# A fixed list of tasks in the place of a planner: block-sparse attention and a gated feed-forward on one core

## The chip, the cores and the metric

The kernel runs on one core of a Trainium2 chip. The core has five engines that work side by side, each through its own instructions in order: TensorE (PE, matrix products, with its weight loads shown as PEld), VectorE (DVE), ScalarE (ACT), GpSimd (POOL) and SyncE (SP, which here issues most of the DMAs). They meet only through semaphores. The metric is the device time of the program in microseconds: the median of 3 runs is 301.85 us (301.69 to 302.9).

## The reference

The input is `q`, `k`, `v` of 4 batches, 8 heads, 768 positions and 64 dimensions, in float32. The positions are cut into 24 blocks of 32. A block of queries sees its own block and the two neighbours, the first and the last block, and three sampled blocks; the first and last block of queries see all.

```python
scores = scale * np.matmul(q, k.transpose(0, 1, 3, 2))
mask = np.abs(blk_i - blk_j) <= window
mask = mask | (blk_i == 0) | (blk_j == 0) | (blk_i == n_blocks - 1) | (blk_j == n_blocks - 1)
for qb in range(n_blocks):
    for kb in sampled_blocks[qb]:
        mask[qb * block:(qb + 1) * block, kb * block:(kb + 1) * block] = True
scores = np.where(mask, scores, -1000000000.0)
attn = np.exp(scores - np.max(scores, axis=-1, keepdims=True))
attn = attn / (np.sum(attn, axis=-1, keepdims=True) + 1e-09)
x = np.matmul(attn, v)          # then (3072 tokens) x (512)
h = x @ w_in                    # 512 -> 2048
g = h * (1.0 / (1.0 + np.exp(-beta * h)))
out = (g @ w_out).astype(np.float32)
```

## The kernel before

The work is cut into tasks: one function each that issues a few instructions on one engine. A task is known by a name, and the numbers behind the name say which piece it is.

**Attention.** The 22 middle blocks of a batch are taken two at a time: 11 pairs a batch, 44 pairs in all, numbered 0 to 43 (`n`). A pair goes through these tasks:

- `kg`, `kn` gather the keys that the pair sees into the tile `KG` (POOL; `kn` on POOL or DVE). `KG` has 3 buffers.
- `vv`, `vg` gather its values into `VG` with DMAs that SP issues; `pick` and `pickv` do it for the sampled blocks of pairs 0 to 3 with PE, because the values are not yet in DRAM.
- `sc` computes mask and scores on PE (`emit_sm` L849, `emit_ss` L862: small products that use quarters of the array, "32-column tiles"). It takes two of the eight PSUM banks.
- `mx` (DVE, L884) takes the maxima, `ex` (ACT, L892) the exponentials and their sums, one task for each of two heads' halves.
- `hl` or `rc` (DVE) invert the sums. From pair 11 on `nrm` (POOL, L915) multiplies the exponentials by them; pairs 0 to 10 put the factor in later (`rs`, L953, L986).
- `tp` transposes on PE (L929), `ptv` copies the result out of PSUM. From pair 31 on one DMA on SP, `tpd` (L933), does both.
- `av` multiplies by the values (L953 and L971 up to pair 15, L963 from pair 16), and `xv` writes the result into `xT`, the feed-forward's input.

The first and last blocks of a batch go through `gs`, `gm`, `ge`, `gr`, `gn`, `gt`, `gptv`, `gav`, `gx` in the same way (L1026 to L1097). Before a batch's pairs, `ldV`, `ldK`, `ldQ` load its data in halves, `cast` turns batch 0's into float16, `trK`, `trQ` (L632) transpose keys and queries with 12 products of 64 columns for two heads, and `evK`, `evQ` copy them out of PSUM.

**Feed-forward.** The tokens are taken in eight groups (`G`) of 256, 256, 256, 512, 512, 512, 512 and 256. `h` (L1155) makes one of 16 slices of the hidden layer for a group, `tanh` (ACT, L1161) and `stt` (DVE, L1166) the gate, `y` (L1182) a quarter of the second product for 128 tokens, `oe` (ACT) copies the result out, `od` writes it to DRAM. The weights come in by POOL's DMAs `win` and `wout`. The gate's results `g` have two buffers; the second one, `g1`, is also lent to the values of pairs 4 to 7.

**The order.** `Plan.run` (L65) is a planner: it follows the dependencies with a duration for each task, and whenever an engine is free it takes the ready task of the lowest rank (its priority and a tuned correction, `OFFSET`). It also chooses the engine of a task that may run on two, and the PSUM bank of a task that opens one. The instructions are then written in the planned order, each engine's in that order. What the planner got wrong shows as an engine that waits: an engine never passes its next instruction by. When PE goes from products that use the whole array to products that use parts of it, or back, it first empties the array; the planner knows this as `CHANGE`.

The names that the change touches: `QV` (L260: what the load of the queries waits for), `TWO` (L268: from which pair on two pairs' scores are one task), `emit_tr` (L628), the casts (L538), `w_in`'s loads (L557), `emit_kg` (L703), the place of `g` (L1146), and the last eviction (L1200 to L1207).

## Time and profile before

| | |
|---|---|
| median of 3 runs | 301.85 us (301.69 to 302.9) |
| the profiled execution: its time, and its span | 302.9 us, 302.9 us |
| busy: PE, DVE, ACT, POOL | 279.5, 237.5, 218.6, 170.0 us |
| instructions: PE products, DVE, ACT, POOL | 4109, 556, 641, 513 |
| moved by DMA | 47.55 MB, of which 11.27 MB by POOL's queue |

The profiled execution is the slowest of the three runs. PE's busy time is modelled: products run into one another, so a slice in which PE is "full" need not be one in which the products follow each other as fast as they can. How fast they can is seen from the start of one to the start of the next. The same holds in small for the other engines: an instruction's last tenth of a microsecond lies under the next one's start.

### The profile page before, as it was taken

The page shows a single profiled execution, that of the slowest core. Times are in us where ns is not written, and L with a number is a line of the kernel's source. Part 1 is how long each engine was busy: PE and PEld are TensorE (multiplying, and loading weights), DVE is VectorE, ACT ScalarE, POOL GpSimd, SP SyncE. Part 2 cuts the span into 40 slices and gives each one's busy share as a digit, 9 for nine tenths or more (in the row PEclk, how much of TensorE's full clock was granted, in tenths as well). Part 3 has the DMA queues.
Part 4 walks back from the last instruction along what each step waited for, and adds up shares of the span by engine and source line. Part 5 has one row for each costly group of instructions (what it writes and reads, how often), then busy time and mean ns, then how long its engine had stood idle before and what let it go on. Part 6 is the DMA issues. An engine that isn't in the chain of part 4 may idle for free.

```text
span 302.9 us, 11451 instructions
## 1 busy us (share of the span) xinstructions
PE 279.5 (92%) x4109; PEld 173.8 (57%) x4109; DVE 237.5 (78%) x556; ACT 218.6 (72%) x641; POOL 170.0 (56%) x513
## 2 busy tenths in 40 slices
PE   2599879999998799999999999999999999999993
PEld 1465668758846576665556555545554544555671
DVE  5848987999899998999999739999888834762150
ACT  3357657888789598799889749896787768763360
POOL 5057995034579957899777538677976654000000
PEclk9999957999999999999999999999999999999999
DMA  7999999979978852299933643248465446541102
GB/s 248 365 294 171 205 232 231 228 142 265 213 126 167 181 192 72 84 173 162 237 99 106 202 154 106 67 110 167 120 158 119 126 106 181 137 121 53 53 36 69
DMA packets 57170, 47.55 MB, mean 157 GB/s; under 512 B 19733, under 2 KB 53142, under 8 KB 57114
## 3 DMA queue, kind: packets, MB, share of 16 engines
q1 hardware_dynamic: 44736, 35.48, 41.3%
q0 software_dynamic: 12320, 11.27, 24.7%
q8 instruction: 32, 0.52, 0.7%
q14 instruction: 24, 0.20, 0.2%
q10 hardware_dynamic: 58, 0.07, 0.1%
HBM read 45.23 MB, written 9.44 MB: 180 GB/s over the span
## 4 chain that ended last, share of the span: by engine, by line
PE 49%; DVE 23%; issue 7%; ACT 6%; POOL 6%; DMA 5%; POOLq 2%; SPq 0%; DVEq 0%; ACTq 0%
PE bank L1155 17%; PE bank L1182 14%; DVE ST L884 5%; PE bank L825 4%; DVE g L1166 4%; PE bank L929 3%; POOL KG L710 3%; DMA g<-in_k_dram 3%; DVE SG L1040 3%; POOL PP L915 2%; PE bank L963 2%; PE bank L971 2%; ACT PP L892 2%; PE bank L632 2%; ACT t L1161 2%
## 5 line engine op out<-in xcount | busy, mean ns | idle before, releaser
L1155 PE MATMUL bank<-xT,w_in_sb 128*128 128x256 f16 (+1 forms) x512 | 93.8, 330 | 1.5 <-DVE g L1166 1.5
L892 ACT ACTIVATE PP<-bank,ST 128x256 f16<-128x256 f32 x176 | 81.9, 482 | 15.1 <-DVE ST L884 10.1
L1182 PE MATMUL bank<-w_out_sb,g 128*128 128x512 f16 x384 | 92.0, 379 | 0.0
L1161 ACT ACTIVATE t<-bank,beta_sb 128x512 f16<-128x512 f32 (+1 forms) x128 | 71.0, 595 | 15.7 <-PE bank L1155 10.4
L915 POOL TENSOR_SCALAR PP<-PP,ST 128x256 f16<-128x256 f16 x132 | 63.4, 499 | 30.8 <-DVE ST L909 29.2
L1166 DVE SCALAR_TENSOR_TENSOR g<-t,bank 128x512 f16<-128x512 f16 (+1 forms) x128 | 67.0, 547 | 16.3 <-ACT t L1161 15.8
L1155 PEld LDWEIGHTS <-w_in_sb 128*128 128x128 f16 x512 | 54.4, 115 | 28.1 <-issue 4.1
L710 POOL COPY KG<-KT 128x64 f32 x264 | 52.4, 249 | 25.6 <-PE bank L862 10.5
L884 DVE TENSOR_REDUCE ST<-bank 128x2 f32<-128x512 f32 x88 | 57.6, 680 | 4.2 <-PE bank L862 3.8
L1182 PEld LDWEIGHTS <-g 128*128 128x128 f16 x384 | 35.0, 98 | 37.4 <-issue 3.5
L892 ACT ACTIVATION_READ_ACCUMULATOR PP<-bank,ST 128x1 f32 x176 | 37.4, 212 | 0.0
L1061 POOL TENSOR_SCALAR PG<-PG,SG 128x768 f16<-128x768 f16 x13 | 13.1, 1010 | 24.4 <-ACT PG L1049 15.2
L334 ACT ACTIVATE osb<-bank 128x512 f32<-128x512 f32 (+1 forms) x24 | 14.2, 590 | 16.1 <-PE bank L1182 16.0
L330 DVE COPY PT<-bank 128x1024 f16<-128x1024 f16 x30 | 20.4, 683 | 3.8 <-PE bank L929 3.6
L330 DVE CAST xT<-bank 64x256 f16<-64x256 f32 (+1 forms) x35 | 14.6, 418 | 9.9 <-PE bank L963 6.8
L929 PE MATMUL bank<-identity,PP 128*128 128x128 f16 x248 | 20.4, 225 | 1.2 <-ACT KT L328 0.6
L963 PEld LDWEIGHTS <-VG 128*128 128x128 f16 x448 | 16.1, 98 | 9.2 <-issue 4.3
L1049 ACT ACTIVATE PG<-bank,SG 128x384 f16<-128x384 f32 x32 | 18.3, 589 | 4.2 <-DVE SG L1042 3.6
L929 PEld LDWEIGHTS <-PP 128*128 128x128 f16 x248 | 16.2, 101 | 6.0 <-issue 1.1
L963 PE MATMUL bank<-PT,VG 128*128 128x64 f16 x448 | 17.5, 193 | 2.2 <-DMA PT<-PP 1.5
L330 POOL COPY KG<-KT 128x384 f32<-128x384 f32 (+3 forms) x43 | 16.6, 411 | 1.3 <-PE bank L862 1.3
L328 ACT CAST xT<-bank 64x256 f16<-64x256 f32 (+1 forms) x30 | 11.3, 375 | 8.2 <-PE bank L1089 3.9
(119 smaller groups left out, 317.9 us busy)
## 6 DMA issues: line engine op xcount, KB each, us to landing
VG<-VT SPq DMA_DIRECT2D x220, 32.0 KB, 2.6
VG<-VT SPq DMA_DIRECT2D x32, 192.0 KB, 2.7
out_dram<-osb SPq DMA_DIRECT2D x20, 256.0 KB, 2.1
RV<-in_v_dram POOLq DMA_DIRECT2D x6, 384.0 KB, 6.6
RK<-in_k_dram POOLq DMA_DIRECT2D x6, 384.0 KB, 6.2
VT<-Vn SPq DMA_DIRECT2D x3, 768.0 KB, 3.4
RQ<-in_q_dram POOLq DMA_DIRECT2D x6, 384.0 KB, 6.3
w_in_sb<-in_moe_w_in_dram POOLq DMA_DIRECT2D x8, 256.0 KB, 8.8
```

The costliest lines, as they stand in the source:

```text
L330: (nc.vector if eng == "DVE" else nc.gpsimd).tensor_copy(out=out, in_=in_)
L710: nc.gpsimd.tensor_copy(out=kg32[:, g, :, (SR + r) * W:(SR + r + 1) * W], in_=kt32[:, :, bass.ds(vals[3 * g + r], W)])
L884: mx[n, u] = add(f"mx{n}.{u}", "DVE", 0.6, lambda n=n, u=u, sb_=sb_: nc.vector.tensor_reduce(out=sb_[:, 0, 2 * u:2 * u + 2], in_=bank(("S" ...
L892: nc.scalar.activation(out=pb[:, u, g, :], in_=bank(("S", n, u))[:, g * 256:(g + 1) * 256], func=AF.Exp, bias=sb_[:, 0, 2 * u + g:2 * u + ...
L915: (nc.vector if eng == "DVE" else nc.gpsimd).tensor_scalar(out=pb[:, u, g, :], in0=pb[:, u, g, :], scalar1=sb_[:, 2, 2 * u + g:2 * u + g + ...
L929: nc.tensor.transpose(out=o[:, s * P:(s + 1) * P], in_=pb[:, u, g, c * P:(c + 1) * P], identity=identity)
L963: nc.tensor.matmul(o[:, (g * NHP + hp) * 2 * BLK:(g * NHP + hp + 1) * 2 * BLK], lhsT=vgb[:, g, c, hp * P:(hp + 1) * P], rhs=pt[:, g, c, :, ...
L1049: nc.scalar.activation(out=pg[:, :].rearrange("x (j p) -> x j p", j=J)[:, :, hf * hw_:(hf + 1) * hw_], in_=bank(("GS", m, hf))[:, 0:S // 2 ...
L1155: nc.tensor.matmul(o[:, 0:TW], lhsT=w_in_v[:, c, f // 4, f % 4, :], rhs=xT[:, c, c0:c0 + TW], start=(c == 0), stop=(c == NHP - 1))
L1161: lambda G=G, f=f, TW=TW, tt=tt: nc.scalar.activation(out=tt[:, 0:TW], in_=bank(("H", G, f))[:, 0:TW], func=AF.Tanh, bias=0.0, scale=beta_ ...
L1166: lambda G=G, f=f, TW=TW, tt=tt, gg=gg: nc.vector.scalar_tensor_tensor(out=gg[:, f, 0:TW], in0=tt[:, 0:TW], scalar=1.0, in1=bank(("H", G, ...
L1182: nc.tensor.matmul(o[:, :], lhsT=gg[:, f, s * P:(s + 1) * P], rhs=w_out_sb[:, f, :], start=(f == 0), stop=(f == N_FFC - 1))
```

## The change

The planner is gone. In its place stands a list, `ORDER`, of 1,727 words: all tasks in the order of writing, with the engine behind the name where a task may run on two (`:A` ACT, `:D` DVE, `:G` POOL) and the PSUM banks where it opens some (`:02`). `Plan.run` only reads the list. Durations that the planner used were also edited in many tasks; they have no effect on the program any more, and those lines are left out below.

With the list come these edits:

- Six `fill` tasks: products of zeros in float32 on PE, with no reader (6, 1, 4, 1, 1 and 2 products, each 128 rows by 256 columns), into a bank that is free at that point.
- Batch 0's casts write two heads side by side, so that its `trK`, `trQ` are 6 products of 128 columns that use the whole array. A cast may run on ACT: 3 of the 8 do.
- `QV`: the load of the queries no longer depends on the first copies of the values. In the list its second half, `ldQ0.1`, stands behind `vtab0.1` and `vtab0.0` on SP.
- `TWO` goes from 33 to 11: from pair 11 on, two neighbouring pairs of a batch have their masks and scores as one task (15 such tasks in the place of 5), which takes four banks at once.
- The register loads of the first four `kg` are tasks of their own, ahead (`kl0` to `kl3`).
- `win`: eight loads of one of the four row groups by half of the columns, in the place of two row groups by a quarter. `h` waits for the four of its half.
- `g` of group 1 lies beside that of group 0 in the first buffer, group 2's in the second. `VG`'s two halves of a pair lie apart.
- A list of row numbers that nothing read (8 POOL, 4 PE and 1 DVE instructions) is gone.
- The last eviction is one instruction on ACT; it was split between ACT and DVE.
- Other engines by the list: `ptv` 21 on DVE and 10 on ACT (before 30 and 1), `nrm` 27 on POOL and 6 on DVE (33 and 0), `xv` without the first eleven pairs 23 on DVE and 38 on ACT (35 and 26), `evK` 1 on DVE and 15 on ACT (4 and 12), `vres` 6 on DVE and 3 on POOL (9 and 0), `kn` 13 on DVE and 31 on POOL (17 and 27).

```diff
+ORDER = """
+sbl iota ldV0.1 ident ldK0.1 ldV0.0 id32 ldK0.0 ldQ0.0 idx kl0 mask.0 kl2 warm mask.1 selc srow kl3 fill6:1 selb0:0
+mask.2 castK0.3:A selb1:1 kl1 table vperm0.1 maskb:2 trK0.3:3 castK0.2:D vtab0.1 selw0 vperm0.0 fill1:5 trK0.2:4 selw1
+evK0.2:A maskc vtab0.0 sel16.4 sel16.3 ldQ0.1 castK0.0:A sel16.2 castK0.1:D fill4:5 trK0.0:4 sel16.1 trK0.1:2 sel16.5
...
+evQ0.1:A kn2:D vg2.2 kg0 evQ0.0:A vg0.2 kn1:D pick1.0:3 vg2.1 vg0.0 castQ0.3:A castQ0.2:D kg2 vg0.1 trQ0.2:2 beta
+trQ0.3:0 evQ0.2:D pick0.0:5 evQ0.3:A pickv1.0:D touch2 wout3.1 pickv0.1:D sc0:02 touch1 pickv0.0:A win1.0 sc1:36 mx0.0
...
+ex5.0 kg7 gm0 sc6:43 pickv2.0:A ge1 av2:0 hl4 win0.3 mx6.1 ge0 tp3:1 kn9:G rs2:D ldV1.0 xv1.0 ex6.1 sc7:26 gr0 vv8
+mx6.0 tp4:5 gn0:G ptv3:A gr1 kn10:G vg5.5 mx7.0 gt0:3 ex6.0 vg7.2 ldK1.1 mx7.1 vg5.3 xv2.0 gn1:G ex7.0 vg8.5 hl6
+fill2:7 gs2:1740 vg6.1 kn8:G gptv0 ptv4:A vg5.4 tp5:2 kg8 gm2 vg7.3 av3:3 ex7.1 vg5.2 vg5.1 av4:5 hl5 ge2 vg6.0 gm3
+win1.3 gt1:6 vg6.6 kg9 vg9.2 rs3:A trK1.1:1 gr2 rs4:A vg6.4 trQ1.0:7 xv3.0 ge3 xv4.0 tp6:3 gptv1 ldQ1.1 h0.1:5
...
+mx20.1 av18:1 vg20.5 tp19:5 vg19.6 mx21.1 tanh2.6 h2.11:4 vg19.3 tanh2.4 stt2.6 y1.0.1 kg24 vg22.3 ex21.1 ptv19:D
...
+y7.1.3 oe7.1 od7.1ACT od7.1SP
+"""
...
     def run(self):
...
+        by = {t.name: t for t in self.tasks}
+        full = dict(A="ACT", D="DVE", P="PE", G="POOL", S="SP")
         order = []
...
+        for word in ORDER.split():
+            name, _, place = word.partition(":")
+            if name.startswith("fill"):
+                k, i = int(name[4:]), int(place)
+                order.append(Task("fill", "PE", 0.43 * k, lambda k=k, i=i: self.fill(k, i)))
...
+            t = by[name]
+            t.eng = full[place[0]] if place and place[0] in full else next(iter(t.on))
...
-    QV = (0, 2)
+    QV = (0, 0)
...
-    TWO, TWOP = 33, 1
+    TWO, TWOP = 11, 1
...
+    def emit_fill(k, i):
+        for _ in range(k):
+            nc.tensor.matmul(banks[i][:, 0:256], lhsT=heat, rhs=heat[:, :].rearrange(
+                "x (a m) -> x a m", a=1).to_broadcast([P, 2, P]), start=True, stop=True, skip_group_check=True)
...
+                    if b == 0:
+                        for j in range(J):
+                            nc.tensor.transpose(out=o[:, j * P:(j + 1) * P],
+                                                in_=mixed(s16)[:, j, hp * P:(hp + 1) * P], identity=identity)
+                        return
...
-        gi = (G + (sizes[0] < 8)) % NG if G or sizes[0] >= 8 else 0
-        gc = TW if G == 1 and sizes[0] < 8 else 0
+        gi, gc = ((0, 0), (0, 256), (1, 0), (0, 0), (1, 0), (0, 0), (1, 0), (0, 0))[G]
...
-                te.emit, te.on = lambda ob=ob, G=G, s=s: scale_on(
-                    "ACT", ob[:, 0:256], bank(("Y", G, s))[:, 0:256], 0.5), {"ACT": 0.35}
-                tf = add(f"of{G}.{s}", "DVE", 0.35, lambda ob=ob, G=G, s=s: scale_on(
-                    "DVE", ob[:, 256:512], bank(("Y", G, s))[:, 256:512], 0.5), deps=list(te.deps), prio=te.prio,
-                    closes=(("Y", G, s),))
```

More of the change, by code (lines that the diff above doesn't have):

```diff
@@ L2 @@
-import heapq
 from contextlib import ExitStack
@@ L65, in run @@
     def run(self):
-        tasks = self.tasks
-        attention_left = sum(1 for t in tasks if t.opens and not t.moe)
-        succ = {}
-        need = {}
-        for t in tasks:
-            need[t] = len(t.deps)
-            for d in t.deps:
-                succ.setdefault(d, []).append(t)
-        readers = {}
-        for t in tasks:
-            for b in t.closes:
-                readers[b] = readers.get(b, 0) + 1
-        ready_at = {t: 0.0 for t in tasks}
-        engines = sorted({e for t in tasks for e in t.on})
@@ L80, in run @@
-        free = {e: 0.0 for e in engines}
-        waiting = {e: [] for e in engines}
-        ring_at = hw_at = 1.0
-        lanes = [0.0] * 8
-        issued = 0
-        tiling = 0
-        off = {t: t.prio + self.OFFSET.get(t.name, self.OFFSET.get(t.name.split(".")[0], self.OFFSET.get(t.kind, 0.0)))
-               for t in tasks}
-        def rank(t, e):
-            young = now - ready_at[t] < self.YOUNG[e] - 1e-9
-            return off[t] + (self.KEEP if e == "PE" and t.tiling != tiling else 0.0) + (self.YIELD if young else 0.0)
@@ L214, in run @@
+        assert sum(t.name != "fill" for t in order) == len(self.tasks) and all(b in self.bank for t in order for b in t.opens)
         return order
@@ L553 @@
     THR = 4.5
-    for fq in range(4):
-        fs = slice(fq * FQ * P, (fq + 1) * FQ * P)
-        for c in range(0, 4, 2):
-            t_win.append(add(f"win{fq}.{c // 2}", "POOL", 0.6, lambda c=c, fs=fs: nc.gpsimd.dma_start(
-                out=w_in_sb[:, c:c + 2, fs], in_=w_in_r[:, c:c + 2, fs]),
-                deps=[touch[fq // 2]], prio=-50 + 0.2 * fq + 0.05 * c, dma=1.3, bulk=THR))
+    for f in range(2):
+        fs = slice(f * D_FF // 2, (f + 1) * D_FF // 2)
+        for c in range(NHP):
+            t_win.append(add(f"win{f}.{c}", "POOL", 0.6, lambda c=c, fs=fs: nc.gpsimd.dma_start(
+                out=w_in_sb[:, c, fs], in_=w_in_r[:, c, fs]),
+                deps=[touch[f]], prio=-50 + 0.4 * f + 0.05 * c, dma=1.5, bulk=THR))
     for c in range(4):
@@ L840, in emit_vres @@
                 copy_on(eng, o, i.to_broadcast([BLK, 2, 2, D_MODEL]))
-            vres = add(f"vres{n}", {"POOL": 2.1, "DVE": 0.62}, None, emit_vres,
+            vres = add(f"vres{n}", {"POOL": 2.1, "DVE": 0.72}, None, emit_vres,
                        deps=vg[n - p] + ([av[vlast(n)]] if vlast(n) >= 0 else []), prio=pr)
@@ L920 @@
         if not late:
-            nrm[n] = add(f"nrm{n}", {"POOL": 1.85, "DVE": 0.8}, None, emit_nrm, deps=[rc], prio=pr - 0.5)
+            nrm[n] = add(f"nrm{n}", {"POOL": 1.75, "DVE": 1.9}, None, emit_nrm, deps=[rc], prio=pr - 0.5)
         def emit_tp(n=n, pb=pb):
```

388 lines of the change are left out of this document (182 added, 206 removed).

## The prediction

> **What bounds the kernel now.** I read the slices of the page first, then the sums over longer stretches.
>
> ```profile
> PE   2599879999998799999999999999999999999993
> DVE  5848987999899998999999739999888834762150
> ```
>
> PE is full from the third slice on, but for a dip before 40 us and another near 100 us. DVE is nearly as full up to slice 32. The sums show where each engine loses:
>
> ```profile
> 28.43:38.67 10.24, 8.15 (x257) 6.11 (x255) 9.56 (x25) 7.54 (x30) 10.12 (x38) 1.00 1.16 200
> 38.67:48.91 10.24, 9.37 (x171) 7.47 (x172) 8.22 (x23) 5.95 (x23) 9.58 (x32) 0.50 1.13 233
> 50.00:80.00 30.00, 30.00 (x542) 22.71 (x540) 28.92 (x83) 24.84 (x71) 10.36 (x22) 1.00 1.05 211
> 95.00:110.00 15.00, 11.38 (x258) 8.58 (x257) 14.70 (x32) 11.14 (x37) 12.04 (x35) 1.00 0.84 202
> 110.00:140.00 30.00, 29.90 (x595) 19.70 (x590) 28.72 (x67) 26.66 (x89) 25.31 (x76) 1.00 0.50 110
> 115.00:250.00 135.00, 132.02 (x1965) 74.86 (x1964) 116.07 (x257) 109.32 (x335) 99.41 (x293) 1.00 0.55 132
> ```
>
> Columns: stretch, length, busy time of PE, PEld, DVE, ACT, POOL, granted clock, DMA share. Half a clock over 10.24 us costs PE 5.1 us of work. From 95 to 110 us PE stands for 3.6 us while DVE is busy 14.70 of 15. So up to 115 us PE, DVE and ACT share the bound; DVE was busy 0.96 of 50 to 80 and of 110 to 140 us. Behind 115 PE stands for only 3.0 of 135 us: there PE's own work is the bound.
>
> **The change part by part.** I cut the list where 13 tasks `y` are written (ahead of `y1.0.1`), and compare with the old kernel at 115 us. First the start of the stage:
>
> ```profile
> 18.37 1.07 DVE L538 CAST RQ<-g 128x768 f16<-128x768 f32 x2 [0.21 <-DMA g<-in_q_dram]
> 21.21 0.86 PE L632 MATMUL bank<-identity,RQ 128*64 128x128 f16 x24
> 23.43 0.33 PE L849 MATMUL bank<-maskr,ones 64*32 64x320 f16 x8
> 24.13 2.48 DVE L884 TENSOR_REDUCE ST<-bank 128x2 f32<-128x512 f32 x4 [1.05 <-PE bank L862]
> 25.32 0.47 ACT L892 ACTIVATE PP<-bank,ST 128x256 f16<-128x256 f32 x1
> 25.77 0.47 ACT L892 ACTIVATE PP<-bank,ST 128x256 f16<-128x256 f32 x1
> ```
>
> The last queries land just ahead of 18.37 us. The same six loads and two writes lie ahead of them on SP, so I leave that landing where it is; `QV` gains nothing, since `ldQ0.1` now stands behind `vtab0.0`, which waits for the same copy. One cast on each of DVE and ACT makes the queries ready at about 19.0. In the old order their transposes stood behind picks on PE until 21.21; in the list they come at once and the pick after. So the stage begins at 19.0, where the old first scores came at 23.43. All in front of it (first fills, casts on ACT, whole-array transposes, `kl`, the dropped row list) I cost at nothing: the landing hides it. If that cover went, the fill of six would be a debt: on one engine everything behind it waits.
>
> How long is the stage? ACT's part, counted from the list, with the rows of ACT:
>
> ```profile
> L892 ACT ACTIVATE PP<-bank,ST 128x256 f16<-128x256 f32 x176 | 81.9, 482 | 15.1 <-DVE ST L884 10.1 <-POOL PP L915 1.6 <-DVE ST L909 1.5
> L892 ACT ACTIVATION_READ_ACCUMULATOR PP<-bank,ST 128x1 f32 x176 | 37.4, 212 | 0.0
> L1161 ACT ACTIVATE t<-bank,beta_sb 128x256 f16<-128x256 f32 x64 | 28.6, 488 | 10.4 <-PE bank L1155 5.8 <-DVE g L1166 3.8 <-PE bank L862 0.2
> L1049 ACT ACTIVATE PG<-bank,SG 128x384 f16<-128x384 f32 x32 | 18.3, 589 | 4.2 <-DVE SG L1042 3.6 <-DVE SG L1057 0.3
> L328 ACT COPY KT<-bank 128x768 f16<-128x768 f16 x12 | 9.6, 817 | 6.4 <-PE bank L632 6.4
> L328 ACT COPY PT<-bank 128x1024 f16<-128x1024 f16 x1 | 1.0, 1020 | 0.0
> L334 ACT ACTIVATE osb<-bank 128x512 f32<-128x512 f32 x23 | 13.8, 599 | 13.3 <-PE bank L1182 13.1
> L328 ACT CAST xT<-bank 64x256 f16<-64x256 f32 x22 | 8.1, 367 | 4.3 <-DVE xT L330 3.8
> ```
>
> Two exponentials start 0.45 us apart with a read of the sum between them (0.482 + 0.212 = 0.694), so each instruction hides 0.12 of the one before; I take that off every mean. Then: 42 `ex` of two at 0.45 each, 38.1; 38 `tanh` at 0.37, 14.1; 12 `ge` at 2 x (0.47 + 0.09), 13.4; 14 `evK`, `evQ` at 0.70, 9.8; 9 `ptv` at 0.90, 8.1; 3 `oe` at 0.48, 1.4; 22 small evictions between 0.25 and 0.48, some 7. Sum 92. DVE has about as much: its largest groups are 44 `mx` at 0.60 (four in 2.48, the last 0.68) and 37 `stt`, and my count of the whole is 92 also. At the share of 0.95 that DVE held, 92 becomes 96.8, and the cut stands at 19.0 + 96.8 = **115.8 us**. The share cannot pass 1 (111 us); it could be as low as 0.74, ACT's own share of 95 to 110 us (143 us), when the engines wait for one another; it is nearest to the long stretches. One `nrm` in this stage is now on DVE, which no row shows; it lies between nothing and POOL's 2.0 (four at 0.499):
>
> ```profile
> L915 POOL TENSOR_SCALAR PP<-PP,ST 128x256 f16<-128x256 f16 x132 | 63.4, 499 | 30.8 <-DVE ST L909 29.2 <-DVE SG L1057 1.3
> ```
>
> How much PE has done at the cut: the rows of PE up to 115 us, and prices from the chain of waits, where products follow each other:
>
> ```profile
> L1155 PE MATMUL bank<-xT,w_in_sb 128*128 128x256 f16 x188 | 25.4, 282 | 1.5 <-DVE g L1166 1.5
> L1182 PE MATMUL bank<-w_out_sb,g 128*128 128x512 f16 x64 | 15.8, 380 | 0.0
> L929 PE MATMUL bank<-identity,PP 128*128 128x128 f16 x128 | 11.2, 231 | 1.2 <-ACT KT L328 0.6 <-POOL PP L915 0.3 <-DVE g L1166 0.3
> L862 PE MATMUL bank<-KG,QT 64*32 64x256 f16 x272 | 6.9, 278 | 0.0
> L1069 PE MATMUL bank<-identity,PG 128*128 128x128 f16 x36 | 3.0, 220 | 0.4 <-POOL PG L1061 0.4
> L1026 PE MATMUL bank<-KT,QT 64*32 64x384 f16 x48 | 1.6, 328 | 0.0
> ```
> ```profile
> 50.03 1.31 PE bank L1155 x12
> 51.68 0.49 PE bank L971 x32
> 54.48 0.21 PE bank L849 x8
> 54.69 0.22 PE bank L862 x16
> 56.34 0.45 PE bank L929 x8
> 58.95 0.45 PE bank L1026 x16
> 283.13 1.73 PE bank L1182 x8
> ```
>
> Old at 115: 47 `h` (188 by 4), 16 `y`, 16 `tp`, 17 pairs' scores, 6 `gt`, 3 `gs`. List at the cut: 39, 13, 20, 22, 10, 6, and (counted in the same view) four `av` and a `gav` more. More work: 4 x 0.45 + 5 x 0.34 + 4 x 0.34 + 3 x 0.45 + 4 x 0.49 + 0.8 = 9.0; less: 8 x 0.44 + 3 x 0.865 = 6.1. PE is **2.9 us ahead**. (0.34 is scores without the switch below; `gt` is six transposes of the eight in 0.45.)
>
> Next the switches between whole array and parts:
>
> ```profile
> 57.06 1.89 PE L1182 MATMUL bank<-w_out_sb,g 128*128 128x512 f16 x8
> 58.88 0.52 PE L1026 MATMUL bank<-KT,QT 64*32 64x384 f16 x16
> ```
>
> Eight `y` products that take 1.73 us elsewhere take 1.82 before a switch: 0.09. Behind the cut the list has 33 switches where PE's old order has 66 behind 115 us, since two pairs' scores are one task: **-3.0 us**. Against it, a pair of scores takes four banks at once and wants two gathers done, with three `KG` buffers; PE's own work hides that as long as `h` and `y` stand ahead of it.
>
> Waits behind the cut: of the old 3.0 us I take 1.0 off, since the 13 transposing DMAs and 302 gathers still share SP's queue in order; bounds -3.0 and +3.0. POOL hands over six `nrm` but takes three `vres` and four `kn`, and win's loads keep their bytes: nothing for either.
>
> The end:
>
> ```profile
> 298.33 0.38 ACT L334 ACTIVATE osb<-bank 128x256 f32<-128x256 f32 x1 [2.86 <-PE bank L1182]
> 298.74 0.42 DVE L336 TENSOR_SCALAR osb<-bank 128x256 f32<-128x256 f32 x1 [6.39 <-ACT osb L334]
> ```
>
> The two halves of the split eviction ran one after the other (0.83 us); one at 0.60 saves **0.2**.
>
> Sum: 302.9 + 0.8 (cut at 115.8, not 115) - 2.9 - 3.0 - 1.0 - 0.2 = 296.6 us, against the profiled 302.9. That execution lies 1.05 above the median, so I predict **295.6 us**.
>
> **The rivals.** *The clock drops again (0.22).* In the old kernel it fell with PE busy 8.15 of 10.24 us, while 11.38 of 15 later did no harm; so it isn't busy time alone. Between `pick2.0` and `h0.1` the list has 11.8 us of ACT's work (12.4 at 0.95) and on PE four `tp`, three `av`, two `sc`, a `gs`, the two fill products, some 8.3 us with the switches: as thin as the stretch that lost the clock. Half a clock over 10.24 us takes 5.1 us, of which the slack there (some 1.5) hides a part: +3.5, 299.1 us. [...]
>
> *Slower: three full engines wait for one another (0.18).* Before the cut ACT, DVE and, with 20 `kg` and 8 `nrm`, POOL have some 90 us each, so each in-order wait on one delays all. It decides at the share: at 0.88 the cut lies at 123.5, 7.7 us later, and the median at 303.3; at 0.85 it is 307. For it speaks that ACT never held more than 0.89 (26.66 of 30) over 30 us; against it, that ACT then waited for PE and DVE.
>
> *The list runs nearly as planned (0.10):* share 0.99 and no waits behind the cut: 3.9 and 2 us off, 289.7. *No difference (0.08):* the share is 0.90, 121.2, and the waits stay: 302.0.
>
> **How the numbers follow.** The forecast has 0.42, for 292 to 299.5. The range 288.5 to 303.5 reaches from the list nearly as planned to the point where the slower case begins. A measurement of this kernel tells 0.5% (1.5 us). Faster by more than that: 0.42 + 0.10 + most of the clock's 0.22, 0.70; within: 0.11; slower: 0.19.
>
> **What would show it.** First scores near 20.5 us; DVE and ACT both above 0.9 up to 115 us, `y1.0.1` near 116; a granted clock of 1.00 from 20 us on; about 103 switches; the last `av` some 30 us of `h` and `y` before the end, where the old one lay 50 before it. The prediction is wrong if PE waits behind 115 us, or if ACT and DVE stand in turn before it.

## The result, and the profile after

The kernel with the list is slower. Over 18 executions of each, its median is 307.19 us (302.74 to 310.25) and that of the kernel before 301.81 us (299.68 to 303.51); the ratio is 1.0118 with a 95% interval of 1.0079 to 1.0157. The prediction was 295.6 us, faster. The ratio leaves out executions that lie more than 1.5% above the fastest of their kernel, which the median beside it counts; where a kernel scatters as widely as this one, the two differ. The profiled execution took 309.33 us, 2.1 above the median, and has a span of 307.6 us; in the executions of the two kernels whose span is on record the time is 1.7 to 1.9 us longer than the span.

First the slices of the kernel after (40 slices of 7.7 us; the third row is the granted clock):

```profile
PE   5899778987999989999969999999999989999994
DVE  5679889995999979889948896765376637764220
PEclk9999799997999999999979999999999999999999
```

PE has dips in slices 5 and 6, 10 and 21, three of them in the slices where the clock falls, and DVE's row has more gaps than before. Then the sums over the two parts that the prediction cut the kernel into, from the transposes of the last queries (19.0 us) to `y1.0.1` (122.6 us), and from there on:

```profile
19.00:122.60 103.60, 93.22 (x2042) 69.21 (x2043) 92.81 (x242) 94.34 (x303) 74.35 (x228) 0.97 0.89 182
122.60:302.00 179.40, 173.74 (x1962) 99.61 (x1961) 118.81 (x254) 126.38 (x352) 82.89 (x239) 0.99 0.51 124
38.40:49.60 11.20, 8.81 (x256) 7.15 (x256) 9.76 (x32) 10.90 (x36) 8.37 (x23) 1.00 1.12 206
71.81:75.22 3.41, 3.41 (x36) 2.47 (x42) 2.10 (x7) 2.30 (x5) 0.68 (x2) 0.50 1.21 230
157.14:160.55 3.41, 3.41 (x23) 1.58 (x21) 2.52 (x6) 2.21 (x4) 1.56 (x4) 0.50 1.20 177
```

The first part takes 103.6 us (predicted 96.8), with ACT busy 94.34 of it, 0.91. The third row is the thin stretch in which the prediction feared for the clock: it kept 1.00. Instead the clock fell to a half for 3.41 us at a time, at 34.3, at 71.8 and at 157.1 us: 10.24 us in all behind the transposes of the queries, as long as the one stretch of the kernel before. What PE waited for, longest sums first:

```profile
PE bank L936 <- DMA VG<-VT: 4.8, 3, 2.8
PE bank L944 <- issue: 3.9, 2, 2.5
PE bank L334 <- DVE se L378: 3.2, 1, 3.2
PE bank L944 <- DMA VG<-VT: 1.4, 2, 1.1
```

Columns: us in total, times, longest. L936 and L944 are the products with the values, `av`; `DMA VG<-VT` are the gathers of the values, `vg`, that SP issues. In the kernel before, no wait of PE for them was among the seven largest. Behind the cut PE stands for 5.7 us (179.40 less 173.74), 4.8 of them for gathers; the old kernel stood for 3.0 us from 115 us on. `L334`, a fill, stands at the very start, ahead of the landing of the queries. The chain of waits says the same (start, length, what):

```profile
68.81 2.46 issue
...
104.32 1.38 SPq L782
105.80 0.54 SPq L782
107.83 3.00 DMA VG<-VT
...
143.28 0.59 SPq L782
143.97 1.71 DMA VG<-VT
...
149.63 1.34 SPq L782
151.07 0.49 SPq L782
152.12 4.60 DMA VG<-VT
```

`SPq` is SP's own time to issue a DMA. So two things are new on the chain: SP's queue, with the gathers that come out of it, and stops of PE that the profile gives to no other engine ("issue"). PE's timeline shows both kinds:

```profile
68.38 0.43 PE L944 MATMUL bank<-PT,VG 128*64 128x32 f16 x17
71.27 0.40 PE L944 MATMUL bank<-PT,VG 128*64 128x32 f16 x15 [2.46 <-issue]
...
156.99 0.91 PE L936 MATMUL bank<-PT,VG 128*128 128x64 f16 x16 [2.84 <-DMA VG<-VT]
```

The first is in the middle of a task, after 17 of 32 equal products that all have their inputs. Each of the two ends less than a microsecond ahead of a stretch of half a clock.

### The profile page after: what moved, and what is told of

Its sections match the earlier page's. It is cut to its first block, busy times and chain, and to the rows that moved or that the text cites. A ratio compares the mean times of both kernels' runs of the same rounds, so it can differ in the third digit from the quotient of the medians.

```text
span 307.6 us, 11337 instructions
## 1 busy us (share of the span) xinstructions
PE 282.4 (92%) x4087; PEld 179.0 (58%) x4087; DVE 223.5 (73%) x537; ACT 230.3 (75%) x667; POOL 163.7 (53%) x498
## 4 chain that ended last, share of the span: by engine, by line
PE 60%; DMA 10%; DVE 9%; ACT 9%; issue 5%; SPq 5%; POOL 1%; POOLq 0%; DVEq 0%; ACTq 0%
PE bank L1128 22%; PE bank L1155 20%; ACT PP L865 5%; PE bank L936 4%; DMA VG<-VT 4%; SPq L782 3%; DVE ST L857 3%; DMA xT<-in_v_dram 3%; DMA g<-in_q_dram 2%; PE bank L902 2%; PE bank L597 2%; PE bank L834 2%; PE bank L1043 2%; PE bank L821 2%; ACT PG L1023 1%
## 5 line engine op out<-in xcount | busy, mean ns | idle before, releaser
L1128 PE MATMUL bank<-xT,w_in_sb 128*128 128x512 f16 (+1 forms) x512 | 99.8, 333 | 0.3 <-ACT PP L865 0.2
L1139 DVE SCALAR_TENSOR_TENSOR g<-t,bank 128x512 f16<-128x512 f16 (+1 forms) x128 | 68.1, 550 | 39.1 <-ACT t L1134 37.9
L1134 ACT ACTIVATE t<-bank,beta_sb 128x512 f16<-128x512 f32 (+1 forms) x128 | 71.8, 590 | 25.5 <-PE bank L1128 18.7
L888 POOL TENSOR_SCALAR PP<-PP,ST 128x256 f16<-128x256 f16 x108 | 50.4, 484 | 38.4 <-DVE ST L882 22.6
L682 POOL COPY KG<-KT 128x64 f32 x264 | 51.0, 243 | 25.8 <-PE bank L834 12.7
L306 POOL COPY KG<-KT 128x384 f32<-128x384 f32 (+3 forms) x55 | 20.7, 406 | 22.8 <-PE bank L834 18.3
L936 PEld LDWEIGHTS <-VG 128*128 128x128 f16 x448 | 16.6, 99 | 12.3 <-DMA VG<-VT 6.2
L936 PE MATMUL bank<-PT,VG 128*128 128x64 f16 x448 | 17.9, 194 | 5.5 <-DMA VG<-VT 4.8
L304 ACT CAST xT<-bank 64x256 f16<-64x256 f32 (+1 forms) x42 | 15.6, 371 | 7.6 <-PE bank L936 4.8
L902 PE MATMUL bank<-identity,PP 128*128 128x128 f16 x248 | 19.1, 222 | 1.4 <-ACT PP L865 0.5
L310 ACT ACTIVATE osb<-bank 128x512 f32<-128x512 f32 x24 | 14.1, 602 | 7.8 <-PE bank L1155 7.8
L1014 DVE TENSOR_REDUCE SG<-bank 128x1 f32<-128x384 f32 x32 | 16.2, 548 | 3.9 <-PE bank L1000 2.3
L306 DVE COPY PT<-bank 128x1024 f16<-128x1024 f16 x21 | 14.3, 681 | 6.1 <-PE bank L936 4.3
```

Source lines behind the costliest of these rows:

```text
L306: (nc.vector if eng == "DVE" else nc.gpsimd).tensor_copy(out=out, in_=in_)
L682: nc.gpsimd.tensor_copy(out=kg32[:, g, :, (SR + r) * W:(SR + r + 1) * W], in_=kt32[:, :, bass.ds(vals[3 * g + r], W)])
L888: (nc.vector if eng == "DVE" else nc.gpsimd).tensor_scalar(out=pb[:, u, g, :], in0=pb[:, u, g, :], scalar1=sb_[:, 2, 2 * u + g:2 * u + g + ...
L902: nc.tensor.transpose(out=o[:, s * P:(s + 1) * P], in_=pb[:, u, g, c * P:(c + 1) * P], identity=identity)
L936: nc.tensor.matmul(o[:, (g * NHP + hp) * 2 * BLK:(g * NHP + hp + 1) * 2 * BLK], lhsT=vgb[:, g, c, hp * P:(hp + 1) * P], rhs=pt[:, g, c, :, ...
L1128: nc.tensor.matmul(o[:, 0:TW], lhsT=w_in_v[:, c, f // 4, f % 4, :], rhs=xT[:, c, c0:c0 + TW], start=(c == 0), stop=(c == NHP - 1))
```

## The experiments

The ratios are against executions of the kernel before on the same chip in the same call; kernels of one call can be compared with each other, and a blank line parts the calls.

```
kernel                median us (lowest, runs)  ratio   95% interval
vtab_early            306.50 (303.0,  4)        1.0181  1.0089 to 1.0273
no_fills              305.11 (304.1, 10)        1.0119  1.0074 to 1.0164
old_order             304.01 (301.8, 10)        1.0059  1.0016 to 1.0103
sc_apart              305.94 (301.9,  4)        1.0156  1.0064 to 1.0247

after_again           307.75 (303.1, 12)        1.0052  1.0008 to 1.0095
fewer_gathers         301.01 (299.0, 12)        0.9931  0.9896 to 0.9965
no_kq1_loads          307.09 (304.6,  6)        1.0113  1.0049 to 1.0178
vg0_pool              301.20 (297.4,  6)        0.9893  0.9817 to 0.9970

gav_later             307.91 (305.0,  6)        1.0153  1.0106 to 1.0201
vg0_pool_nofill       300.72 (299.3, 12)        0.9928  0.9899 to 0.9957
vg0_pool_nofill_gav   300.33 (298.9, 12)        0.9924  0.9895 to 0.9953
old_order_pool        313.09 (309.1,  6)        1.0300  1.0243 to 1.0357

sp_tiny               300.81 (299.0, 13)        0.9963  0.9921 to 1.0006
old_order_pad         307.01 (303.1, 12)        1.0116  1.0074 to 1.0157
pool_apart            304.60 (302.6, 12)        1.0074  1.0037 to 1.0111

no_fills_again        303.98 (301.4, 12)        1.0042  1.0003 to 1.0082
one_less              299.33 (298.0,  6)        0.9895  0.9844 to 0.9946
window_small          303.28 (301.1, 12)        1.0023  0.9986 to 1.0059
```

**Is it the list or the edits?** `old_order` has all the edits, but the old planner's order written as a list, with scores of two pairs merged from pair 33 on as before, and no fills.

```diff
-    TWO, TWOP = 11, 1
+    TWO, TWOP = 33, 1
 # ORDER: the tasks in the planner's order, its engines and banks; no fill
```

> All edits of the change but the list: the old planner's order, engines and banks (TWO at 33, no fills), written out as a list. If the order is what cost the 5 us, this is at 300 to 303 and its lead of the gathers is that of the old kernel, 10 to 18 us between 90 and 130 us. Rival: the edits themselves cost (w_in's halves, the place of the gate's results, the layout of the values): 305 or more.

It is 0.6% slower than before, half of what the list's kernel is by the ratio and a third by the medians (1.8 of 5.4 us). So the edits alone give nothing and cost a little. That the list costs the rest is what the medians say; the ratios don't settle it, since the list's kernel unchanged has 1.0118 in one call and 1.0052 in another (`after_again`, below). A stop of 3.36 us lies in this kernel's profile too, and again in the middle of equal products:

```profile
32.77 0.39 PE L834 MATMUL bank<-KG,QT 64*32 64x256 f16 x13
36.52 0.29 PE L834 MATMUL bank<-KG,QT 64*32 64x256 f16 x3 [3.36 <-issue]
```

**A late value table.** My first theory for the waits was that batch 1's values reach DRAM too late, so that the gathers start late. `vtab_early` moves their load and their permutation ahead.

```diff
-... ge2 vg6.0 gm3 win1.3 gt1:6 ...     tanh0.1 ldV1.1 vg9.3 ...     evQ1.1:A permV1.1 wout1.1 ...
+... ge2 vg6.0 gm3 ldV1.1 win1.3 ...    tanh0.1 vg9.3 ...            mx9.1 permV1.1 av5:5 ...
```

> The list with two words moved: the load of the second half of batch 1's values stands ahead of the last load of the first weights on POOL, and its copy on DVE (permV1.1) some 6 us earlier. Theory G (late gathers: SP stood from 53.6 to 69.7 us behind the write of batch 1's values to DRAM, and from there to 157 us each pair's last value gather was issued only 1.5 to 5 us ahead of its product): the gathers begin again at 63 to 64 us in the place of 69.7, the stops of PE at 109 (1.3), 144 (0.7) and 152 to 157 us (3.0, and the half clock behind it 1.7) go, and the median falls from 307.2 to 302 to 304. Theory B (late instruction blocks: PE stops at instruction 704 and 2240 because the block of 256 that follows had not landed): those two stops of 1.6 and 2.6 us stay, ACT still idles 2 us at each, and the median stays within 1.5 of 307.

The gathers did begin again earlier, at 63.5 us in place of 69.7, but nothing was gained (306.5 us), and PE still waits 3.6 us for gathers. From pair 12 to 23 the last gather was issued the same 2 to 5 us ahead of its `av` as in the list's kernel. This theory fell.

**SP's queue.** The next theory: SP issues a pair's seven gathers at 0.47 us each, with register loads between, some 4 us a pair, while the list wants a pair's values about every 4 us: pair 12's `av` starts at 100.0 us and pair 19's at 127.6, one each 3.9 us (in `old_order` at 98.2 and 133.6, one each 5.1). A pair's gathers must wait for the `av` four pairs earlier (`VG` has four buffers), and once SP is behind it doesn't catch up. SP's timeline of the kernel after, around 120 us:

```profile
103.39 8.57 SPq L782 DMA_DIRECT2D VG<-VT  x14
112.06 0.38 SPq L1182 DMA_DIRECT2D out_dram<-osb  x1
112.53 18.37 SPq L782 DMA_DIRECT2D VG<-VT  x31
131.00 0.37 SPq L1182 DMA_DIRECT2D out_dram<-osb  x1
131.46 7.74 SPq L782 DMA_DIRECT2D VG<-VT  x12
```

31 gathers in a row, one each 0.59 us: 4.1 us for seven. How far the last gather of a pair is issued ahead of the pair's `av`, worked out from the trace (us):

```
pair             12   13   14   15   16   17   18   19   20   21   22   23
old_order      14.7 12.4  8.8  8.5  8.3  9.3  6.7  5.9  6.3  7.6  9.1  5.5
after           4.4  4.1  4.7  1.5  3.8  3.4  3.3  3.3  4.4  1.8  4.8  4.4
vg0_pool        6.2  5.4  7.1  4.7  7.8  5.5  5.4  5.2  9.2  4.8 10.5  4.6
```

A gather takes 2.4 to 2.9 us to land (median), so at a lead of 3 or 4 us any delay stops PE. The same leads stand in a shorter execution: 1.5 to 5.7 us in the profile of `gav_later` (below), which took 305.0 us. In the old order the `av` came later: pair 18's at 127 us and pair 22's at 155, against 121 and 139 in the list. So SP had less to issue in the same time, 92 gathers from 85 to 160 us against 108 in the list, and it stood behind ACT for the writes of the output (`old_order`, the same stretch):

```profile
SPq L1182 <- ACT osb L310: 9.3, 3, 5.5
```

The list moves `av` forward, and SP's speed does not move.

Two experiments took load off SP; `after_again` is the list's kernel unchanged, for their call. `fewer_gathers` leaves three of the six sampled gathers out for pairs 10 to 27:

```diff
+            def emit_vg(..., left=n in range(10, 28) and k_ >= len(list(moves())) - 3):
+                if left:
+                    return
```

> The changed kernel once more, unaltered, as the reference beside the others of this call. Theory B (late instruction blocks): PE stops again behind instruction 704 and 2240, 1.3 to 1.5 us after the block's packet has landed. Theory G (SP full of gathers): between av10 and av23 the last value gather of a pair is again issued less than 6 us ahead of its product. Median 305 to 308.

> For pairs 10 to 27 three of the six gathers of sampled value blocks are left out, so that half of these blocks hold an earlier pair's values: 54 DMAs less on SP (at some 0.46 us each 25 us between 70 and 170 us). Theory G: the last gather of these pairs is issued 8 us or more ahead of its product, PE's waits for VG (6.2 us in the profile of the changed kernel) fall below 1, the median falls by 4 to 6 us against the reference of this call. Theory B: PE's stops behind instruction 704 and 2240 lie before these pairs and stay; -1.5 us at most.

`vg0_pool` leaves nothing out. From pair 12 on POOL issues the gather of the pair's window, the one of 192 KB, and its word stands some ten tasks behind the `av` that frees the buffer:

```diff
-    NBP, ODP, RP = 99, (), 0
+    NBP, ODP, RP = 12, (), 0
 # ORDER, pair 12 for example
-... permV2.0 y0.1.1 nrm13:G ex14.0 vg12.0 stt1.7 ...
+... av8:7 tanh0.9 mx11.0 vg11.4 ex11.1 vg11.1 h0.11:3 gr4 stt0.9 vg11.2 rs8:A vg12.0 tp9:5 ...
```

> From pair 12 on the one gather of the neighbouring value blocks (192 KB) is issued by POOL in the place of SP, written some ten tasks behind the product that frees its buffer. Theory G: SP issues six in the place of seven DMAs a pair, the lead of the gathers grows by 0.4 to 0.5 us a pair, to 5 us or more at av16 to av20; -1 to -3 us. Rival: POOL stands in order at each of these (its buffer, 0.75 us to issue), and gathers of keys and norms come late by as much: +2 us or more. Theory B: no change.

Against 307.75 us of `after_again`, `fewer_gathers` has 301.01 and `vg0_pool` 301.20; by the ratios the two gain less, 1.2 and 1.6% (3.7 and 4.8 us), which is still clear of the noise. The list's kernel (unchanged) waited for gathers as before:

```profile
PE bank L936 <- DMA VG<-VT: 4.5, 3, 2.8
```

In `vg0_pool` that wait is gone from PE's list, and SP itself now waits for the buffers, that is for PE (SP's waits from 85 to 160 us):

```profile
SPq L782 <- PE bank L936: 6.3, 5, 3.1
SPq L782 <- PE bank L944: 3.1, 2, 1.7
```

Those are 9.4 us; in the list's kernel the same waits sum to 2.3. PE's busy time in the 75 us from 85 on, of `after_again` and then of `vg0_pool`:

```profile
85.00:160.00 75.00, 69.96 (x1211) 47.65 (x1210) 64.69 (x151) 64.65 (x199) 58.10 (x174) 0.98 0.62 141
```
```profile
85.00:160.00 75.00, 73.19 (x1292) 50.46 (x1292) 70.65 (x159) 68.13 (x211) 68.70 (x191) 1.00 0.63 144
```

PE gains 3.2 us of work, and the half clock behind the stop at 155 us is gone with the stop. The part behind the cut fell from 185.1 us to 178.0.

Is SP limited by the number of DMAs, or by their bytes? Three runs ask this, two of them on the list without fills (`no_fills_again`). `one_less` leaves the last sampled gather out from pair 12 on: one DMA and 32 KB of a pair's 384. `window_small` keeps all seven and makes the window's gather 32 KB in place of 192. `sp_tiny` starts from `vg0_pool` without fills, and puts a DMA of 4 bytes on SP for each pair, in the place of the gather that went to POOL.

```diff
 # one_less
+            def emit_vg(..., left=n >= 12 and k_ == len(list(moves())) - 1):
+                if left:
+                    return
 # window_small
-                    vgb[0:3 * BLK, :, 1, :],
+                    vgb[0:(3 if n < 12 else 1) * BLK, 0:(2 if n < 12 else 1), 1, :],
 # sp_tiny
+                if n >= 12 and eng == "SP" and k_ == len(vg_moves) - 6:
+                    nc.sync.dma_start(out=tiny[0:1, n, :], in_=vt[0:1, 0:2])
```

> The changed kernel without its fills, as the reference of this call: 305 as before, SP waits less than 3 us for free buffers between 85 and 160 us, and the last gather of pairs 15 to 19 is issued 1.5 to 4 us ahead of its product.

> no_fills, and from pair 12 on the last of the six sampled gathers (32 KB) is left out: that block holds an earlier pair's values. SP issues six in the place of seven DMAs a pair as in vg0_pool, and 352 in the place of 384 KB. If slots are the limit: as vg0_pool_nofill, 4 to 5 us below the reference. If the bytes of SP's queue are: a twelfth of them, -0.5 us.

> no_fills, and from pair 12 on the gather of the neighbouring value blocks moves one block (32 KB) in the place of six (192 KB); the other five hold an earlier pair's values. SP issues seven DMAs a pair as in the changed kernel, and 224 in the place of 384 KB. If bytes are the limit: 4 to 5 us below the reference. If slots are: -1 us at most.

> vg0_pool_nofill, and SP issues one more DMA of 4 bytes per pair from pair 12 on, behind its first sampled gather: the number of SP's DMAs is that of the changed kernel again, the 192 KB stay with POOL. If the number is the limit (theory G in the form of issue slots of 0.47 us), the lead of the gathers falls back to 2 to 4 us at av15 to av19 and the median goes from 300.7 back to 305 or more. If it was the large transfer in SP's own queue, the median stays within 1.5 of 300.7.

One DMA less gains 4.7 us (303.98 to 299.33; one execution of `no_fills_again` took 1517 us, and the ratio leaves it out); 160 KB less, at the same number, gains 0.7 (303.28), which these runs can't tell from nothing. By these two it is the number. `sp_tiny` doesn't fit: at seven DMAs it should have lost most of what `vg0_pool_nofill` won, some 4 us, and it lost about 1 (0.4% faster than before in place of 0.7, with intervals that overlap). Its small DMAs take a shorter slot:

```profile
118.60 0.28 SPq L782 DMA_DIRECT2D tiny<-VT  x1
118.98 1.25 SPq L785 DMA_DIRECT2D VG<-VT  x3
120.28 0.28 SPq L782 DMA_DIRECT2D tiny<-VT  x1
```

From start to start 0.37 us, a fifth less than a gather's 0.47: one slot of seven, so it explains little. That no `av` waits for a tiny DMA, and that POOL issues the window's gather earlier than SP would, may be the rest. Which it is stays open, and with it whether SP's slots are the whole of the limit.

**Does POOL's help make the old order faster too?** `old_order_pool` has the same move in the planner's order.

```diff
-    NBP, ODP, RP = 99, (), 0
+    NBP, ODP, RP = 12, (), 0
 # on old_order; ORDER: the window's gathers ten tasks behind the av, as in vg0_pool
```

> The edits in the old planner's order, with the neighbouring gather of pairs 12 and on on POOL as in vg0_pool. Theory G says that the old order was not held by SP (its gathers led by 8 to 18 us up to 130 us and by 4 to 6 behind it, waits for VG 1.0 us): -1 us against old_order (304), 303. If moving the gather is a gain of its own in any order: -4 or more, 300.

It is the slowest of all, 313.09 us. PE now waits for POOL:

```profile
PE bank L1042 <- POOL PG L1034: 5.1, 4, 2.0
```

In the old order POOL's queue is where the gathers hurt: `PG` is the result of `gn`, and PE's transposes `gt` stand waiting for it. The Trainium skill, "Perfetto Trace Analysis", section "DMA Optimizations", says that where issuing is the limit rather than the transfers, spreading DMAs over the engines that can issue them may help. The two runs show both sides of that "may": 4.8 us won in the list by the ratios and 6.5 by the medians, and a ratio that rose by 2.4% in the old order (1.0059 to 1.0300).

**Stops within a task.** The trace shows that PE's program itself is fetched by DMA, in packets of 16 KB on a queue of its own:

```profile
q8 instruction: 32, 0.52, 0.7%
```

One packet for each 256 instructions of PE, its products, weight loads and semaphore instructions together. The longest stops that no engine explains lie at the same counts, at 448 and each 256 further (times here run from the start of the last instruction ahead of a stop, 0.2 to 0.3 us more than the idle time in the rows): in the list's kernel at 704 (32.26 to 33.87 us) and 2240 (68.63 to 71.27), in the kernel before at 960 (37.11 to 39.54), in `old_order` at 704. The packets landed at 32.49 and 69.71 us in the list's kernel, 1.4 and 1.6 us before PE went on. The profile had put the old kernel's stop down to DVE (2.17 us of it). Not every "issue" is such a stop: the one of 2.0 us in `no_fills` at 152.7 us lies off these counts, ahead of pair 23's `av`, where the other runs wait for gathers. Without fills the same counts fall on other tasks.

```diff
-... fill6:1 ... fill1:5 ... fill4:5 ... fill1:4 ... fill1:1 ... fill2:7 ...
```

> The list without its six fill tasks (15 products, 60 of PE's instructions). Theory B: PE's stops without a semaphore stay at the instruction numbers 448 + 256 k (704, 960, 2240), though other tasks now stand there, 60 instructions further down the list; if the stop of 2.65 us instead stays inside the products av8 (then at number 2181), theory B falls. The clock of the first 18 us goes back to half as in the old kernel, hidden by the landing of the queries: median within 1.5 of 307 by my step that the fills are worth nothing; rival: the fills are worth the clock at 35 us, which then drops for 10 us as in the old kernel: 310.

`no_fills` stops again at 704 (0.3 us) and at 2240 (1.8 us), the latter now within `h` in place of `av`: the place goes by the count, not by the work. Why are the packets late? That stays open; it is not because of the loads of batch 1's keys and queries:

```diff
+                                 (b, nm) not in ((1, 'K'), (1, 'Q')) and nc.gpsimd.dma_start(...)
```

> The four loads of batch 1's keys and queries (384 KB each, issued between 26 and 49 us) are left out, so that batch 1 runs on batch 0's keys and queries; all other work stays. Theory B: with that traffic gone the instruction blocks 2 to 8 land 2.5 to 4 us after their request in the place of 4 to 7.5, PE's stops up to 75 us (4.6 us in sum) fall below 1, ACT's two holes of 2 us go, y1.0.1 starts 4 us earlier (118 in the place of 122.6) and the median falls by 3 to 5 us. Theory G: nothing behind 85 us moves but by what SP gains; -1 us.

That kernel leaves 1.5 MB of loads out and stops just as long (2.4 us at 704, 2.1 at 2240); this expectation was missed. A stop can be moved away, by moving PE's work past the count: `gav_later` writes the product `gav0` behind `gt5` (and `gx0` behind it).

```diff
-... gm4 wout2.0 ge5 gav0:6 kn13:G ...   sc11:05 wout2.1 h0.10:1 gr5 kn14:G hl9 gx0:A ...
+... gt5:1 tanh0.15 stt1.3 gav0:0 vg13.2 ...   vg12.6 stt0.15 kg14 gx0:A ...
```

> The changed kernel with batch 0's gav (48 products, 96 of PE's instructions) moved from before sc11 to behind gt5, 15 us later. Theory B: instruction 2240 now falls into the scores of pairs 12 and 13, 2 to 3 us of work further on, and the block is there: the stop of 2.1 to 2.65 us and ACT's hole of 2.2 us go, the clock keeps whole speed at 70 to 75 us in most runs, and y1.0.1 starts 2 to 4 us earlier than 122. What theory G makes of the end: from pair 10 on SP's gathers set the pace, so PE waits for VG by as much more, and the median falls by less than 1.5 us (306 to 307); if late blocks were the main cause of the loss it falls by 4 (303.5).

The stop at 2240 is gone, and no half clock is left:

```profile
PEclk9999999999999999999999999999999999999999
```
```profile
PE bank L936 <- DMA VG<-VT: 4.9, 4, 2.7
```

The cut came at 118.7 us instead of 122.6 (120.9 in `after_again`), and still the median is 307.91: the part behind the cut takes 184.5 us, and PE waits for gathers as long as ever. One of these waits stops PE from 150.7 to 153.3 us and leaves the clock whole. What is won ahead of a queue that sets the pace is handed back at the queue. Does it pay once the queue is relieved? Two kernels on `vg0_pool`:

```diff
 # vg0_pool_nofill: vg0_pool without fills
 # vg0_pool_nofill_gav: and with gav0, gx0 as in gav_later
```

> vg0_pool without the six fill tasks. By my step that they cost nothing: 301, as vg0_pool. Rival: the nine products from 20 us on stand on PE's path (0.9 us at 23, 34 and 43 us each, modelled) and their 36 instructions bring the block boundaries nearer: 299 to 300.

> vg0_pool without the fills and with batch 0's gav moved behind gt5. Both theories together: without the gathers' limit behind 85 us the 2 to 4 us that the removed stop at instruction 2240 gives in front now reach the end: 2 us or more below vg0_pool_nofill. If B is worth nothing even then: equal to it within 1 us.

300.72 and 300.33 us: 0.4 us, which is within the error. The stops are real and cost PE's time where they stand; in the median of these kernels they decide nothing that could be measured. What the fills cost is not settled: by the ratio nothing (1.0119 and 1.0042 without them in two calls, 1.0118 and 1.0052 with them), by the medians against before 2 to 4 us.

**Merged scores.** The term of -3.0 us stood on fewer switches of PE. `sc_apart` takes the scores of a pair apart again (`TWO` 33), with the second pair's ahead of its maxima; `pool_apart` does so on `vg0_pool_nofill`.

```diff
-    TWO, TWOP = 11, 1
+    TWO, TWOP = 33, 1
-... sc12:4675 ...
+... sc12:46 ... sc13:75 ...
```

> The list with the scores of two pairs as two tasks again (TWO at 33), the second ahead of its own maxima: 121 switches between whole and part array in the place of 103, 43 in the place of 33 behind y1.0.1. My term: 0.09 each, of which the eight before y1.0.1 are hidden behind ACT: +0.9 us, 308.1. Rival: two pairs at a time hold four banks and two gathers of keys, and apart they let the maxima start earlier: -1 us or more, 306.

> vg0_pool_nofill with two pairs' scores as two tasks again (120 switches in the place of 102, 43 in the place of 33 behind y1.0.1). My term of 0.09 each behind the cut: +0.9 us, 301.6; with those in front 302.3. Rival (as sc_apart hinted: 305.9 against 307.8): earlier scores let maxima and exponentials start earlier, -1 us or more, 299.5.

With SP in the way nothing is seen: 305.94 us, inside the spread of the list's kernel. With SP relieved, apart is some 4 us slower (304.60 to 300.72 in two calls; by their ratios, 1.0074 and 0.9928, 1.5%). The 18 more switches of the expectation at 0.09 are 1.6 us of it; the rest has no row.

**Where the edits lose.** The 0.6% of `old_order` might come from where PE's counts fall. `old_order_pad` adds 53 small products with no reader, to shift all counts.

```diff
+fill5:0 ... fill24:0 ... fill24:0
-            nc.tensor.matmul(banks[i][:, 0:256], lhsT=heat, rhs=heat[:, :].rearrange(...), ...)
+            nc.tensor.matmul(banks[i][:, 0:8], lhsT=ones, rhs=ones[:, 0:8], ...)
```

> old_order with 53 empty products (8 columns each, no reader) in front: 5 behind the mask, 24 behind the transposes of the keys and 24 behind the first of the queries, where the old kernel had 106 instructions more. Theory B: the stop goes from behind instruction 704 (3.6 us) to behind 960 (some 2.4 us) as in the old kernel, and the median from 304.0 to 302.5. Rival: the edits cost by something else: 304 or, with some 2 us of empty products in front, 305.

The stops moved (1.3 us at 704, 2.9 at 960), but the kernel got 3 us slower, and the last of batch 0's queries were transposed at 21.7 us in place of 20.4. The pad cost more than it could show. Why the edits in the old order lose 1.8 us stays open.

## Why the prediction was wrong, point by point

By the spans of the two profiled executions, the forecast was 296.6 and the kernel took 307.6: 11.0 us too few. 6.8 of them lie ahead of the cut, 4.2 behind it, and one step of the prediction failed on each side: the share that gave the cut, and the waits behind it.

- **"The stage begins at 19.0": right.** The transposes start at 19.06 us, the first scores at 21.13 (forecast 20.5).

```profile
19.06 0.84 PE L592 MATMUL bank<-identity,RQ 128*128 128x128 f16 x12 [0.55 <-DVE RQ L306]
21.13 0.33 PE L821 MATMUL bank<-maskr,ones 64*32 64x320 f16 x8
```

- **"At the share of 0.95 that DVE held, 92 becomes 96.8": this step failed, +6.8 us, the larger of the two.** ACT was busy 94.3 us in place of 92, and held 0.91. The step lent DVE's share to ACT, whose own best was 0.89 in the same rows (110 to 140 us); with that the sum gives 103.4 us and a cut at 122.4, where 122.6 was measured. That this comes so close is in part luck, as ACT's work was 2.3 us more than counted. The 9.3 us in which ACT stood have two main entries:

```profile
ACT VG L304 <- PE bank L797: 2.4, 2, 1.9
ACT RS L310 <- PE bank L944: 2.2, 1, 2.2
```

In the longer wait of the first entry (1.9 us) ACT stands for a `pick` that PE reaches late, behind the stop at 704, the half clock from 34.3 to 37.7 us and a fill; the second entry lies behind the stop at 2240. In `gav_later`, without the second stop and without half a clock, the part from 19.0 us to the cut is 99.7 us, against 103.6 in the profiled execution and 101.4 in `after_again`. So 2 to 4 us went there, and the other 3 to 5 are work and waits that the share undersized; which waits, no run tells apart. The prediction had no term for PE standing still within a task.

- **"PE is 2.9 us ahead" and "33 switches, -3.0": the counts were right.** PE's work behind the cut, by the same prices, is 168.4 us against the forecast 168.1 (171.0 in the old kernel behind 115 us, less 2.9); the list has 33 switches there and 103 in all by the prediction's count. The price of a switch no run measured alone: in `pool_apart` taking scores apart costs more than its 18 switches at 0.09.

- **"Waits behind the cut: I take 1.0 off; bounds -3.0 and +3.0": this step failed too, and it is the one that the runs turned round.** What is left of the time there when PE's work, its switches and the end are taken off went from 6.5 us to 9.4 where 5.5 was forecast: 2.9 us more than the old, at the upper bound, and 3.9 over the forecast. In PE's own rows: it stands for 5.7 us in place of the old 3.0 (2.0 forecast), and the half clock behind one of these stops takes 1.7. The step saw that 302 gathers share SP's queue in order, and let that stand for "no change". It had to set SP's time per pair (7 x 0.59) against the spacing of `av` in the list. That was nearly there to be read: the kernel before shows SP in its timeline at 45 gathers one each 0.67 us, of which 5 us in all are SP's own waits (0.56 without them),

```profile
130.48 30.01 SPq L810 DMA_DIRECT2D VG<-VT  x45
```

and the list has the order of the readers. The price of that queue as a whole is larger than the step's miss. `vg0_pool` brings the part behind the cut to 178.0 us, 2.8 below the forecast. Its cut lies at 121.8 us, as late as the list's, and still its span of 299.7 us is 3.2 below that of the kernel before. `gav_later` is the reverse: its cut comes 2 to 4 us earlier, and its median gains nothing.

- **The end, -0.2: right.** One eviction of 0.60 us, and 4.35 us from the last `y` to the end in place of 4.6.

- **The median.** The prediction took the span of 302.9 us for the time, and 1.05 us for its distance from the median. With the 1.7 to 1.9 us seen in later executions that time would be about 304.7, which is none of the three runs, and the distance about 2.8. Then the two slips cancel, and the sum stays at 295.6.

**The rivals.** *Three full engines wait for one another* had the sign and nearly the cut (123.5 against 122.6) at 303.3 us. But ACT's two largest waits ahead of the cut were for PE, mostly behind late pieces of PE's own program, and behind the cut it was SP, a fifth engine that it did not count. *The clock drops again* was wrong in its place and in its cause: the thin stretch kept 1.00 with PE busy 8.81 of 11.20 us. All four stretches of half a clock, the old kernel's too, begin within a stop of PE of 1.6 us or more or less than a microsecond behind it; `gav_later`, whose stops at these counts are 1.1 us at most, has none, but it kept the clock through a stop of 2.65 us for a gather too, and in `no_fills_again` the clock fell at 43.6 us with no stop of PE over 0.9 us in the 18 us ahead. So what makes it fall stays open. Behind 19 us the sum is the same 10.24 us in both kernels, so the clock doesn't explain the difference. *Runs nearly as planned* and *no difference* fell with the waits.

**Was the list worth anything?** With the gathers relieved, yes: `vg0_pool_nofill` is 0.7% faster than before (0.43 to 1.01%), and 1.3% below `old_order` by the ratios to before in their calls (0.9928 against 1.0059). That is a third of the 2.1% that were forecast.

## What to carry to other kernels

When an order is written anew, hold each queue that issues DMAs against it as an engine like the others: its time per issue, times the issues that the new order wants in a stretch, and how far ahead of its reader each is issued; a queue with little room before will not follow when its readers move forward. A queue's load moved to another engine is a gain only where that engine has room: the same move was worth 1.6% here in one order and cost 2.4% in the other. And what is won ahead of the queue that sets the pace is not won.

## What the runs showed of the hardware that was not expected

- **PE's own instructions can be late.** PE stopped at fixed counts (448 and each 256 further), for 2.4 us in the old kernel, 2.6 in the list's and 3.6 in `old_order`. In the two kernels compared they lie in the first 72 us, where the 16 DMA engines were busiest. Wherever PE stopped so, in any of the runs, it went on 1.2 to 1.7 us after the packet had landed. The Trainium skill, "Runtime: NRT & Kernel Launch", section "Instruction fetch mechanics", has the blocks of 256 instructions and calls the cost of crossing into the next "mostly hidden". The size agrees with the trace. The cost doesn't where transfers crowd: 1.6 and 2.6 us for the two longest in the list's kernel, and the profile shows them as "issue", or puts them down to another engine.
- **Half a clock comes in pieces of 3.41 us.** In the profiles of all runs the stretches at 0.50 were 3.41 us long, or two or three times that (6.83 in `no_fills_again`, 10.24 in the kernel before), but for the last one, which the end of the program cuts off.
- **Single executions of one kernel scatter by 2 to 3%.** The list's kernel ran between 302.7 and 312.5 us. `vg0_pool_nofill_gav` scatters less (298.9 to 302.3), `vg0_pool` hardly (297.4 to 304.6). That a lead of 3 or 4 us makes each late transfer count would explain a part, but no run tested it.
